# Decay attention into a mixture of experts: handing the expert weights' nine transfers to the scheduler later

## The chip, the core and the metric

One core of one Trainium2 chip runs the whole kernel. The metric is device microseconds of one execution, as the median of several; lower is better. Engines are called PE (matrix products), DVE, ACT and POOL (element-wise work; only DVE and ACT read PE's accumulators), and SP, which issues every transfer of this kernel.

## What is computed

The input is eight batches of eight heads with 576 positions and 64 channels. First comes causal attention with a decay that is added to the scores:

```python
scores = scale * np.matmul(q, k.transpose(0, 1, 3, 2))
log_f = np.log(np.clip(f, 0.0001, 1.0))
cum = np.cumsum(log_f, axis=-1)
decay = cum[:, :, :, None] - cum[:, :, None, :]
scores = np.where(causal, -1000000000.0, scores + decay)
attn = softmax(scores)            # written out in the reference
out = np.matmul(attn, v)
```

The heads of a batch are joined into x (576 x 512), and four experts follow. Each one is causal attention over x with its own matrices; a gate keeps the best two of four per position:

```python
logits = x @ w_gate               # the two largest, softmax over them: w
q, k, v = x @ wq[e], x @ wk[e], x @ wv[e]
a = softmax(where(causal, -1e9, scale * q @ k.T))
out += mask_e * w * (a @ v @ wo[e])
```

## The kernel before

**Pairs.** The unit of work is a pair: two heads of the decay attention (`a`), or two experts (`m`), for one batch. The order is four `a` pairs of batch 0, then for each batch from 1 on its four `a` pairs and the two `m` pairs of the batch before, and at the end two `m` pairs: 48 pairs. Products are made to nearly full precision out of a high and a low part of each operand, `x = h + l`: ACT writes the rounded copy `h`, and DVE or POOL subtracts it from `x` to get `l`.

**Stages of a pair.** `prep_attn` loads k and q, turns them over on PE (L278), and splits them (ACT L286 into tile `kq`, DVE L287 into `ka`). `max_pass` computes all scores once (L439) for the row maxima (DVE L445, L489), turns the maxima over on PE (L494, tile `mp`), copies them out with ACT (L496, tile `ms`) and sends them by two small transfers into row 68 of `kq` (`copy_bits`, L255). `scores` computes them again with that row (L525, L526), takes exponentials on ACT (L545 to L576), zeroes what lies above the diagonal on POOL (L511, L547, L577) and adds up row sums on POOL (L583 to L586, tile `R`). `attend` is L607; `row_sums` and `apply_rows` divide by the sums and split the result into `xh` (ACT L711) and `xl` (DVE L712). Those feed the experts: `moe_front` (L337), `prep_moe` (L413) and at the end of a batch `project_out` (L734).

**The weights.** `load_weights` (L199) brings the experts' matrices in once, in nine steps: two transfers of wv and the small one of w_gate, two of wk, two of wq (L226), two of wo (L221). Each step loads a staging tile `st`, has ACT copy the high part (L229: `vh`, `kh`, `qh`, `oh`) and POOL subtract for the low part (L230: `vl`, `kl`, `ql`, `ol`).

**The order of the work.** A heap (L792 to L803) hands out the steps of all stages by due time in units of pairs: each stage has a start and an end out of the tables `PLAN`, `HEAD`, `TAIL` and `W`, and its steps are spread between them. In that order the instructions are given to the framework's list scheduler, which then sets each engine's own order by its estimate of when operands are there. The weights' task is L791, with start `W["l0"]` and end `W["l1"]`: step i of nine is due at l0 + (l1 - l0) x i / 9. Every engine then runs its list strictly in order; an instruction that waits holds up all behind it. POOL's `memset` of the maxima's tile (L435) waits until PE has turned over the maxima of two pairs before, since there are two buffers.

Of the kernel before, what the change touches and what calls it, by code (L numbers as in the profile page):

```python
# [21 lines left out]
INV_SCALE = 8.0  # L22


W = dict(d1=-1.62, l0=1, l1=4, c0=-1.39, c1=-1.57, x0=-0.76)
PLAN = {
    "a0": dict(prep=(-1.974, -1.27), vals=(-0.214, -0.256), max=(-0.804, -1.205), scores=(0.003, 0.147), attend=(1.121, 1.748)),
    "a1": dict(prep=(-2, -1.228), vals=(-0.415, 1.126), max=(-0.601, -0.643), scores=(-0.269, 0.973), attend=(1.185, 2.238), sums=(1.749, 1.965), apply=(2.392, 2.449)),
# [26 lines left out]
def tile_decay_attention_moe(ctx: ExitStack, tc, q, k, v, f, w_gate, wq, wk, wv, wo, out):  # L55
# [665 lines left out]
    def project_out(grp, b):  # L721
        yh, yl = grp["yh"], grp["yl"]
        wh, wl = wts["o"]

        for blk in [4, 0, 1, 2, 3] if b % 2 else range(4):
            po = ptile(ps_x, "x", f"po{b}_{blk}")
            n = 0
            for a in range(NEP):
                if blk < 4:
                    lh, ll = (y[a][:, 128 * blk : 128 * blk + 128] for y in (yh, yl))  # L730
                else:
                    lh, ll = (y[:, a] for y in last64[0])
                for l, r in ((lh, wh), (lh, wl), (ll, wh)):
                    nc.tensor.matmul(po, l, r[:, a], start=(n == 0), stop=(n == 3 * NEP - 1))  # L734
                    n += 1
            if b < B - 2:
                ob = work.tile([128, DM], F32, tag="outb", name=f"outb{b}_{blk}", bufs=2)
            else:
                ob = xs.tile([128, S], F32, tag="xl", name=f"outb{b}_{blk}")[:, :DM]
            nc.scalar.activation(ob, po, AF.Copy)  # L740
            if blk < 4:
                nc.sync.dma_start(out[b, 128 * blk : 128 * blk + 128], ob)
            else:
                for i in range(2):
                    nc.sync.dma_start(out[b - 1 + i, 512:S], ob[64 * i : 64 * i + 64])
            yield 2.0
# [9 lines left out]
    def task(t0, t1, total, make):  # L756
        tasks.append([t0, len(tasks), t0, t1, total, 0.0, make, None])
# [4 lines left out]
    for i, (kind, b, p) in enumerate(seq):  # L762
# [20 lines left out]
        if p % 2 == 1:  # L783
            task(*at["sums"], 3.0, lambda g=grp, us=us, b=b, kind=kind: row_sums(g, us, b, kind))
            task(*at["apply"], 2.0, lambda g=grp, us=us, b=b, kind=kind, p=p: apply_rows(g, us, b, kind, p - 1))
            if kind == "m":
                task(*at["out"], 10.0, lambda g=grp, b=b: project_out(g, b))
    task(-1.999, W["d1"], 1.0, decay_rows)
    task(W["c0"], W["c1"], 1.0, constants)
    task(W["x0"], W["x0"], 1.0, spread_rows)  # L790
    task(W["l0"], W["l1"], 4.0, load_weights)  # L791
    heap = [tuple(x[:2]) for x in tasks]  # L792
# [31 lines left out]
```

## Time and profile before

| | us |
|---|---|
| median of 3 runs | 768.52 (768.11 to 770.03) |
| the profiled execution's own time | 770.86 |
| its span, first to last instruction | 768.5 |
| PE busy | 726.0 (94% of the span) |
| DVE busy | 586.7 (76%) |
| ACT busy | 471.5 (61%) |
| POOL busy | 406.5 (53%) |

The span is what the trace's times count from; the profiled execution took 2.4 us more than its span, which lie around it. A row of the timeline view gives start, duration, engine, line, what was written from what, and in brackets how long the engine had sat idle and what ended that. SPq rows are issues of transfers, not the transfers themselves. The clock row of this profile prints full speed from the start, so for the first stretch the durations of equal matmuls are the better guide.

### The profile page before, as it was taken

The page shows a single profiled execution, that of the slowest core. Times are in us where ns is not written, and L with a number is a line of the kernel's source. Part 1 is how long each engine was busy: PE and PEld are TensorE (multiplying, and loading weights), DVE is VectorE, ACT ScalarE, POOL GpSimd, SP SyncE. Part 2 cuts the span into 40 slices and gives each one's busy share as a digit, 9 for nine tenths or more (in the row PEclk, how much of TensorE's full clock was granted, in tenths as well). Part 3 has the DMA queues.
Part 4 walks back from the last instruction along what each step waited for, and adds up shares of the span by engine and source line. Part 5 has one row for each costly group of instructions (what it writes and reads, how often), then busy time and mean ns, then how long its engine had stood idle before and what let it go on. Part 6 is the DMA issues. An engine that isn't in the chain of part 4 may idle for free.

```text
span 768.5 us, 16867 instructions
## 1 busy us (share of the span) xinstructions
PE 726.0 (94%) x5704; PEld 592.5 (77%) x5704; DVE 586.7 (76%) x1856; ACT 471.5 (61%) x1151; POOL 406.5 (53%) x770
## 2 busy tenths in 40 slices
PE   4699899999999999999999999999999999999997
PEld 3577589768887788777987778877887879879865
DVE  7678977988688877888778886878777987785733
ACT  5477556767566765676556765667656865555543
POOL 8297644564455564456446544555644564473260
PEclk9999999999999999999999999999999999999999
DMA  8974540544226441365224542265413632202203
GB/s 165 192 146 105 124 107 22 115 92 95 49 49 154 109 109 33 69 147 138 67 53 98 142 110 49 50 144 133 108 33 65 150 88 48 55 19 52 67 15 123
DMA packets 142233, 70.84 MB, mean 92 GB/s; under 512 B 124004, under 2 KB 124484, under 8 KB 142148
## 3 DMA queue, kind: packets, MB, share of 16 engines
q1 hardware_dynamic: 142148, 69.77, 40.3%
q8 instruction: 45, 0.74, 0.4%
q14 instruction: 40, 0.33, 0.1%
HBM read 31.43 MB, written 9.74 MB: 54 GB/s over the span
## 4 chain that ended last, share of the span: by engine, by line
PE 76%; DVE 11%; ACT 4%; DMA 4%; issue 3%; POOL 2%; SPq 0%; DVEq 0%; ACTq 0%
PE pp_m L413 11%; PE ob_a L607 8%; PE pv L337 7%; PE po L734 7%; PE m_a L439 7%; PE s_a L525 6%; PE s_a L526 5%; PE ob_m L607 4%; PE tp_a L278 4%; PE s_m L526 3%; PE s_m L525 3%; PE m_m L439 3%; PE sm_a L650 2%; DVE junk_a L445 2%; DVE ka_a L287 2%
## 5 line engine op out<-in xcount | busy, mean ns | idle before, releaser
L287 DVE TENSOR_TENSOR ka_a<-tp_a,kq 64x288 fp32r<-64x288 f32 x256 | 114.6, 453 | 19.2 <-ACT kq L286 12.6
L286 ACT ACTIVATE kq<-tp_a 64x288 fp32r<-64x288 f32 x256 | 101.1, 403 | 39.7 <-DVE ka_a L287 23.5
L445 DVE CUSTOM_DVE_ANT_0 junk_a<-m_a,mask 128x192 bf16<-128x192 f32 (+2 forms) x192 | 93.5, 487 | 40.8 <-PE m_a L439 22.5
L525 PE MATMUL s_a<-ka_a 128*128 128x320 f32 (+4 forms) x384 | 112.7, 316 | 2.8 <-ACT P_a L545 1.6
L439 PE MATMUL m_a<-kq 128*128 128x320 f32 (+4 forms) x384 | 103.9, 333 | 8.7 <-DVE mxs_a L445 3.9
L526 PE MATMUL s_a<-kq 128*128 128x320 f32 (+4 forms) x384 | 102.2, 298 | 0.5 <-DMA kq<-ms_a 0.5
L420 ACT ACTIVATE kq<-pp_m 64x288 fp32r<-64x288 f32 x128 | 51.8, 405 | 70.9 <-PE pp_m L413 34.8
L547 POOL TENSOR_SCALAR_AFFINE_SELECT P_a<-P_a 128x256 f32<-128x256 f32 x64 | 26.1, 409 | 125.3 <-ACT P_a L545 125.2
L511 POOL TENSOR_SCALAR_AFFINE_SELECT P_a<-P_a 128x128 f32<-128x128 f32 x128 | 42.1, 332 | 82.3 <-ACT P_a L560 80.5
L439 PEld LDWEIGHTS m_a<-kq 128*128 128x128 f32 (+1 forms) x384 | 65.1, 190 | 19.1 <-DVE mxs_a L445 8.0
L525 PEld LDWEIGHTS s_a<-ka_a 128*128 128x128 f32 (+1 forms) x384 | 69.8, 184 | 11.7 <-issue 4.3
L421 DVE TENSOR_TENSOR ka_m<-pp_m,kq 64x288 fp32r<-64x288 f32 x128 | 58.1, 454 | 24.7 <-ACT kq L420 22.2
L583 POOL TENSOR_TENSOR R_a<-P_a 128x448 f32<-128x448 f32 x64 | 73.3, 1145 | 4.2
L526 PEld LDWEIGHTS s_a<-kq 128*128 128x128 f32 (+1 forms) x384 | 69.0, 183 | 2.5 <-DMA kq<-ms_a 0.7
L607 PE MATMUL ob_a<-P_a,va 128*64 128x320 f32 (+1 forms) x512 | 69.2, 412 | 1.0 <-POOL pl L577 1.0
L445 DVE CUSTOM_DVE_ANT_0 junk_m<-m_m,mask 128x192 bf16<-128x192 f32 (+2 forms) x96 | 46.6, 486 | 16.1 <-PE m_m L439 14.2
L525 PE MATMUL s_m<-ka_m 128*128 128x192 f32 (+2 forms) x192 | 56.8, 316 | 0.5 <-ACT P_m L560 0.2
L607 PEld LDWEIGHTS ob_a<-P_a,va 128*64 128x64 f32 x512 | 33.9, 136 | 30.2 <-POOL pl L577 2.3
L584 POOL TENSOR_TENSOR R_a<-R_a,P_a 128x320 f32<-128x320 f32 x64 | 55.0, 864 | 1.0
L526 PE MATMUL s_m<-kq 128*128 128x192 f32 (+2 forms) x192 | 50.6, 295 | 1.9 <-DMA kq<-ms_m 1.8
L439 PE MATMUL m_m<-kq 128*128 128x192 f32 (+2 forms) x192 | 48.0, 310 | 0.0
L337 PE MATMUL pv<-vh,xh_a 128*128 128x260 f32 x160 | 47.6, 297 | 0.0
(190 smaller groups left out, 2065.5 us busy)
## 6 DMA issues: line engine op xcount, KB each, us to landing
ka_a<-kq SPq DMA_DIRECT2D x64, 288.0 KB
kn_a<-in_k_dram SPq DMA_DIRECT2D x64, 144.0 KB
qn_a<-in_q_dram SPq DMA_DIRECT2D x64, 144.0 KB
ka_m<-kq SPq DMA_DIRECT2D x32, 288.0 KB
va<-in_v_dram SPq DMA_DIRECT2D x64, 128.0 KB
out_dram<-outb SPq DMA_DIRECT2D x32, 256.0 KB
kq<-ex SPq DMA_DIRECT2D x94, 9.0 KB
va<-in_v_dram SPq DMA_DIRECT2D x32, 32.0 KB
```

The source lines that it names most:

```text
L286: nc.scalar.activation(hv, src, AF.Copy)
L287: nc.vector.tensor_tensor(lo[:, h, gs], src, hv.bitcast(F32), ALU.subtract)
L337: nc.tensor.matmul(pv[:, :NV], l[c][:, t0 : t0 + 128], r[:, c], start=(n == 0), stop=(n == 3 * KC - 1))
L413: nc.tensor.matmul(pp[:, :HS], w[:, c, es], x[c][:, gs], start=(n == 0), stop=(n == 3 * KC - 1))
L421: nc.vector.tensor_tensor(lo[:, h, gs], src, hv.bitcast(F32), ALU.subtract)
L439: nc.tensor.matmul(dst, qB[0:K, h, i0 : i0 + dst.shape[0]], kB[0:K, h, j0:j1], start=True, stop=True)
L445: nc.vector.tensor_tensor_reduce(jk[:, :n], src, mask[:, MW - n :], 1.0, init, ALU.add, ALU.max, acc)
L525: nc.tensor.matmul(dst, kaf[:, c : c + m], qA[:, h, i0:i1], start=True, stop=False)
L526: nc.tensor.matmul(dst, kqf[0:K, c + h * S : c + h * S + m], qB[0:K, h, i0:i1], start=False, stop=True)
L583: g.tensor_tensor(r[:, h, 128:S], q[:, 320:768], q[:, 768:1216], ALU.add)
L584: g.tensor_tensor(r[:, h, 256:S], r[:, h, 256:S], q[:, 1216:1536], ALU.add)
L607: mm = nc.tensor.matmul(dst[64 * h : 64 * h + 64, c0 : c0 + rhs.shape[-1]], vs[h][0:kp, blk], rhs, start=first, stop=last,)
```

## The change

Two numbers of table `W` change: `l0` from 1 to 1.6, `l1` from 4 to 5.

```diff
-W = dict(d1=-1.62, l0=1, l1=4, c0=-1.39, c1=-1.57, x0=-0.76)
+W = dict(d1=-1.62, l0=1.6, l1=5, c0=-1.39, c1=-1.57, x0=-0.76)
```

So the nine steps are due at 1.60, 1.98, 2.36, 2.73, 3.11, 3.49, 3.87, 4.24 and 4.62 pairs, where they were due at 1.00, 1.33, 1.67 and so on to 3.67. Nothing is added or removed. The scheduler's lists change on every engine well beyond the weights: on PE the first difference is at the 26th row and the last near row 1,870 of some 3,780; behind that all engines' lists are the same.

**First place: SP and ACT in the first pairs.** Tiles are named with stage, pair within its batch and a running number. On SP, ahead of and behind the two transfers of pair 0's row maxima (`kq_111<-ms_a_0`), before:

```order
L226 DMA st_v_540<-in_moe_wv_dram 128x8x64
L255 DMA ka_a_2_354<-kq_113 64x2x576
L306 DMA va_104<-in_v_dram 128x4x64 x2
L311 DMA va_104<-in_v_dram 64x2x64
L306 DMA va_105<-in_v_dram 128x4x64
L255 DMA ka_a_2_354<-kq_113 64x2x576
L306 DMA va_105<-in_v_dram 128x4x64
L311 DMA va_105<-in_v_dram 64x2x64
L226 DMA st_v_600<-in_moe_wv_dram 128x8x64
L255 DMA kq_111<-ms_a_0_303 1x5x128 x2
L226 DMA st_v_659<-in_moe_w_gate_dram 128x4x4
L226 DMA st_k_705<-in_moe_wk_dram 128x8x64
```

and now:

```order
L306 DMA va_104<-in_v_dram 128x4x64
L255 DMA ka_a_2_354<-kq_113 64x2x576
L306 DMA va_104<-in_v_dram 128x4x64
L311 DMA va_104<-in_v_dram 64x2x64
L306 DMA va_105<-in_v_dram 128x4x64 x2
L255 DMA ka_a_2_354<-kq_113 64x2x576
L311 DMA va_105<-in_v_dram 64x2x64
L226 DMA st_v_639<-in_moe_wv_dram 128x8x64
L255 DMA kq_111<-ms_a_0_303 1x5x128 x2
L226 DMA st_v_695<-in_moe_wv_dram 128x8x64
```

One transfer of wv instead of two now stands ahead of the maxima's. On ACT, around the copy of pair 0's maxima (`ms_a_0`) and its first exponentials (`P_a_0`), before:

```order
L286 ACTIVATE kq_114<-tp_a_3_586 64x288
L229 ACTIVATE vh<-st_v_540 128x4x128
L286 ACTIVATE kq_114<-tp_a_3_616 64x288
L496 ACTIVATE ms_a_0_303<-mp_a_0_301 10x128
L229 ACTIVATE vh<-st_v_600 128x4x128
L229 ACTIVATE vh<-st_v_659 128x4x4
L545 ACT_TABLE_LOAD
L545 ACTIVATE P_a_0_316<-s_a_0_318 128x512
L229 ACTIVATE kh<-st_k_705 128x4x128
L545 ACTIVATE P_a_0_316<-s_a_0_333 128x512
```

and now:

```order
L286 ACTIVATE kq_114<-tp_a_3_580 64x288
L286 ACTIVATE kq_114<-tp_a_3_606 64x288
L496 ACTIVATE ms_a_0_303<-mp_a_0_301 10x128
L229 ACTIVATE vh<-st_v_639 128x4x128
L545 ACT_TABLE_LOAD
L545 ACTIVATE P_a_0_316<-s_a_0_318 128x512
L229 ACTIVATE vh<-st_v_695 128x4x128
L229 ACTIVATE vh<-st_v_767 128x4x4
L545 ACTIVATE P_a_0_316<-s_a_0_333 128x512
```

The first `vh` went from ahead of `ms_a_0` to behind it, and the second and third from ahead of the first exponential to between the first and the second.

**Second place: POOL and DVE when batch 0's first results are split.** On POOL, the row sums of pair 3 (`R_a_3`) and the weights' low parts among them, before:

```order
L577 AFFINE_SELECT pl_108<-pl_108 64x128
L584 TENSOR_TENSOR R_a_3_959<-R_a_3_959,P_a_3_958 128x320 x2
L230 TENSOR_TENSOR ol<-st_o_1013,oh 128x512
L585 TENSOR_TENSOR R_a_3_959<-R_a_3_959,P_a_3_958 128x192 x2
L230 TENSOR_TENSOR ol<-st_o_1056,oh 128x512
```

and now:

```order
L577 AFFINE_SELECT pl_108<-pl_108 64x128
L584 TENSOR_TENSOR R_a_3_949<-R_a_3_949,P_a_3_948 128x320 x2
L435 MEMSET mxs_a_2_1301 64x2
L585 TENSOR_TENSOR R_a_3_949<-R_a_3_949,P_a_3_948 128x192
L230 TENSOR_TENSOR ql<-st_q_1020,qh 128x4x128
L585 TENSOR_TENSOR R_a_3_949<-R_a_3_949,P_a_3_948 128x192
L586 TENSOR_TENSOR R_a_3_949<-R_a_3_949,pl_108 64x2x64
L230 TENSOR_TENSOR ql<-st_q_1094,qh 128x4x128
```

A `memset` now stands behind the first two additions, and the two `ql` come where one `ol` was (the two `ol` follow later). On DVE, ahead of the second split (`xl_a_0_1`), before:

```order
L712 TENSOR_TENSOR xl_a_0_0_974<-ot_a_0_632,xh_a_0_0_973 128x576
L287 TENSOR_TENSOR ka_a_1_870<-tp_a_1_997,kq_112 64x288
L694 TENSOR_TENSOR ot_a_1_679<-cp_a_0_1020,ot_a_1_679 128x288
L287 TENSOR_TENSOR ka_a_2_926<-tp_a_2_946,kq_113 64x288
L712 TENSOR_TENSOR xl_a_0_1_1024<-ot_a_1_679,xh_a_0_1_1023 128x576
```

and now:

```order
L287 TENSOR_TENSOR ka_a_1_860<-tp_a_1_987,kq_112 64x288
L445 ISA junk_a_0_946,mxs_a_0_878<-m_a_0_944,mask 128x320
L445 ISA mxs_a_0_878 128x1
L489 TENSOR_REDUCE mxs_a_0_878<-mx_a_0_933 64x2
L712 TENSOR_TENSOR xl_a_0_1_1008<-ot_a_1_671,xh_a_0_1_1007 128x576
```

The second split now follows the last reduction of the maxima `mxs_a_0`, which POOL's `memset` of `mxs_a_2` waits for by way of PE.

## Rows read from the trace of the kernel before

**Rows 1.** Busy time of each engine in stretches of 20 us (windows view): stretch, its length, busy us and instructions of PE, PE's weight loads, DVE, ACT and POOL, then PE's clock row, the share of the 16 transfer engines in use and GB/s.

```profile
0.00:20.00 20.00, 9.12 (x42) 7.38 (x43) 15.13 (x37) 9.92 (x23) 16.80 (x43) 1.00 0.90 167
20.00:40.00 20.00, 13.98 (x51) 10.81 (x51) 10.94 (x40) 9.38 (x21) 5.47 (x9) 1.00 1.07 190
40.00:60.00 20.00, 19.31 (x140) 14.19 (x139) 15.97 (x53) 14.28 (x37) 18.04 (x32) 1.00 0.76 152
60.00:80.00 20.00, 18.86 (x157) 14.09 (x156) 17.45 (x41) 14.01 (x35) 15.88 (x28) 1.00 0.46 104
80.00:100.00 20.00, 15.74 (x117) 11.10 (x117) 18.54 (x54) 12.51 (x30) 10.12 (x19) 1.00 0.51 105
...
120.00:140.00 20.00, 20.00 (x180) 18.11 (x178) 16.41 (x55) 11.16 (x27) 9.71 (x17) 1.00 0.14 32
140.00:160.00 20.00, 18.60 (x162) 13.96 (x158) 18.17 (x58) 14.17 (x37) 13.28 (x26) 1.00 0.55 121
```

**Rows 2.** PE's timeline from 23 to 38 us.

```profile
23.88 0.71 PE L278 MATMUL tp_a<-ident,kn_a 96*128 96x96 f32 x3 [2.18 <-DMA kn_a<-in_k_dram]
...
26.95 0.37 PE L494 MATMUL mp_a<-ident,mxs_a 128*10 128x128 f32 x1 [0.17 <-DVE mxs_a L489]
...
29.08 1.06 PE L439 MATMUL m_a<-kq 128*128 128x192 f32 x3 [1.19 <-ACT ms_a L496]
30.79 0.98 PE L439 MATMUL m_a<-kq 128*128 128x448 f32 x2 [0.65 <-DVE mxt_a L456]
...
37.23 0.58 PE L525 MATMUL s_a<-ka_a 128*128 128x256 f32 x1 [0.58 <-ACT P_a L545]
```

**Rows 3.** ACT's timeline from 27 to 38 us.

```profile
27.95 0.63 ACT L229 ACTIVATE vh<-st_v 128x512 fp32r<-128x512 f32 x1 [2.06 <-DMA st_v<-in_moe_wv_dram]
28.48 0.39 ACT L286 ACTIVATE kq<-tp_a 64x288 fp32r<-64x288 f32 x1
28.77 0.25 ACT L496 ACTIVATE ms_a<-mp_a 10x128 fp32r<-10x128 f32 x1
32.83 0.88 ACT L229 ACTIVATE vh<-st_v 128x512 fp32r<-128x512 f32 x2 [3.81 <-DMA st_v<-in_moe_wv_dram]
35.28 1.28 ACT L545 ACT_TABLE_LOAD   x1 [1.58 <-PE s_a L526]
...
37.59 0.59 ACT L545 ACTIVATE P_a<-s_a 128x512 f32<-128x512 f32 x1
```

**Rows 4.** SP's issues from 21 to 31 us (timeline).

```profile
21.43 0.69 SPq L226 DMA_DIRECT2D st_v<-in_moe_wv_dram  x1
...
29.14 0.60 SPq L226 DMA_DIRECT2D st_v<-in_moe_wv_dram  x1
29.84 1.64 SPq L255 DMA_DIRECT2D kq<-ms_a  x2
```

**Rows 5.** Issues by transfer, with the size of one (transfer view).

```profile
st_v<-in_moe_wv_dram SPq DMA_DIRECT2D x2, 256.0 KB
```

**Rows 6.** DVE's timeline from 77 to 83 us.

```profile
77.08 3.54 DVE L712 TENSOR_TENSOR xl_a<-ot_a,xh_a 128x576 fp32r<-128x576 f32 x1 [0.26 <-ACT xh_a L711]
80.65 1.42 DVE L287 TENSOR_TENSOR ka_a<-tp_a,kq 64x288 fp32r<-64x288 f32 x3
```

**Rows 7.** All executions of the line L712 (source view): count, then the shortest, median and longest in ns.

```profile
L712 DVE TENSOR_TENSOR xl_a<-ot_a,xh_a x32: 742/750/3539, 74.4 to 692.4; 128x576 fp32r<-128x576 f32 x32
```

**Rows 8.** POOL's timeline: one row at 60 us, then 75 to 83 us.

```profile
60.49 0.09 POOL L435 MEMSET mxs_a<- 64x2 f32 x1 [1.09 <-PE mp_a L494]
...
75.98 1.68 POOL L584 TENSOR_TENSOR R_a<-R_a,P_a 128x320 f32<-128x320 f32 x2
77.63 1.26 POOL L230 TENSOR_TENSOR ol<-st_o,oh 128x512 fp32r<-128x512 f32 x1
78.85 1.14 POOL L585 TENSOR_TENSOR R_a<-R_a,P_a 128x192 f32<-128x192 f32 x2
82.13 1.26 POOL L230 TENSOR_TENSOR ol<-st_o,oh 128x512 fp32r<-128x512 f32 x1 [2.14 <-ACT oh L229]
```

**Rows 9.** PE's timeline from 81 to 84 us.

```profile
81.59 0.41 PE L439 MATMUL m_a<-kq 128*128 128x320 f32 x1 [1.16 <-ACT kq L286]
82.22 0.44 PE L278 MATMUL tp_a<-ident,qn_a 96*128 96x96 f32 x3 [0.22 <-DVE ka_a L287]
83.64 0.39 PE L525 MATMUL s_a<-ka_a 128*128 128x256 f32 x1 [0.98 <-ACT P_a L545]
```

**Rows 10.** ACT's timeline from 81 to 82 us.

```profile
81.13 0.41 ACT L286 ACTIVATE kq<-tp_a 64x288 fp32r<-64x288 f32 x1 [3.50 <-DVE ka_a L287]
81.44 0.62 ACT L229 ACTIVATE oh<-st_o 128x512 fp32r<-128x512 f32 x1
```

**Rows 11.** All executions of the small DVE line L672 (source view), as in Rows 7.

```profile
L672 DVE TENSOR_TENSOR zt_a<-rc_a,zt_a x16: 191/196/1153, 63.9 to 685.4; 128x18 fp32r<-128x18 f32 x16
```

**Rows 12.** POOL's timeline at 64 us.

```profile
63.87 1.14 POOL L583 TENSOR_TENSOR R_a<-P_a 128x448 f32<-128x448 f32 x1
```

**Rows 13.** First uses of the weights on PE (source view): after the counts and durations come the start of the first and of the last execution.

```profile
L337 PE MATMUL pv<-vh,xh_a x160: 279/283/388, 98.4 to 722.5; 128*128 128x260 f32 x160
...
L413 PE MATMUL pp_m<-xh_a,qh x128: 290/296/401, 113.5 to 716.0; 128*128 128x288 f32 x128
...
L734 PE MATMUL po<-oh,yh_m x64: 391/398/502, 236.3 to 763.9; 128*128 128x512 f32 x64
```

**Rows 14.** Two matmuls of the same shape in PE's timeline, at 40 and at 100 us.

```profile
40.22 0.57 PE L526 MATMUL s_a<-kq 128*128 128x448 f32 x1
...
100.54 0.37 PE L526 MATMUL s_a<-kq 128*128 128x448 f32 x1
```

## The prediction

> **What bounds the kernel now.** I read the windows view first, to see where PE has time to lose. From 100 us on there is next to none: PE is busy for all of 120 to 140, and 1.4 us short of full from 140 to 160, the worst later stretch of this size until the end of the program comes near [rows 1]. So a saving has to come out of the first 100 us, where PE is idle for 10.9, 6.0, 0.7, 1.1 and 4.3 us of five stretches of 20 [rows 1]. The reader should see two holes in this: one from 20 to 40, where transfers are saturated (190 GB/s, and the share of the engines in use is over 1), and one from 80 to 100, where transfers are at half and DVE is busy 18.5 us of 20. The first 20 us come ahead of all that the change touches.
>
> I read the first hole in the PE timeline and then asked each releaser what held it. PE waits 2.18 us for pair 3's k, which was issued before any weights and is not touched. Then it waits 1.19 us for `ms_a`, 0.65 for a DVE reduction, 0.58 for the first exponential [rows 2]. `ms_a` is the copy of pair 0's maxima on ACT. Its input was turned over on PE at 26.95 and took 0.37, so it was there at 27.32 [rows 2], but ACT started it at 28.77, because ACT had stood 2.06 us on the first transfer of wv, until 27.95, and the weight copy and a queued split came first [rows 3]. That is a weight which nobody reads before 98.4 us [rows 13], standing in front of the work that PE is waiting for.
>
> The second hole has another cause. DVE's split `xl_a` at 77.08 took 3.54 us [rows 6]; the median of its 32 executions is 0.75 [rows 7]. POOL added two-operand tiles without a gap from 75.98 to 79.99 meanwhile, one of the additions being the low part of a weight, `ol` [rows 8], and the split ended 0.63 us after POOL stopped. The small L672, median 0.196, shows the same thing: its longest execution is 1.15 us, starting at 63.9 [rows 11], under a POOL addition from 63.87 to 65.01 [rows 12]. A DVE operation with two operands in SBUF gets little through while POOL runs such operations back to back. Behind that split ACT sat idle for 3.50 us until DVE's next release [rows 10], and PE lost 1.16, 0.22 and 0.98, together 2.36 us [rows 9].
>
> **The change, part by part.** The sum is against the profiled execution, 770.86 us; the median of the runs is 768.52, 2.34 lower, and I carry the difference over unchanged. No instruction is added or removed; only places change.
>
> *The maxima of pair 0.* `ms_a` now stands ahead of all weight copies on ACT. Its input is there at 27.32, so it starts some 1.4 us earlier (28.77 less 27.35, with ACT's queued split done by then). That removes PE's 1.19 us wait [rows 2]. The row then has to reach `kq`: its two transfers were issued at 29.84, behind two wv transfers of 256 KB [rows 4, 5]. One of the two is now behind them. At 190 GB/s [rows 1] 256 KB is 1.38 us, and an issue of 0.69 on SP goes too [rows 4], so the landing moves by about as much as PE does, and the scores follow. I take **-1.2 us**. The ends: 0, if the removed wait comes back one step later (first rival below), and -2.4, if the waits of 0.65 and 0.58 behind it close as well (1.19 + 0.65 + 0.58). I take the row that is directly released, since the other two have releasers of their own: DVE has to reduce what PE makes, and the exponential needs its table load of 1.28 us whatever the weights do [rows 3].
>
> One rule speaks against this part. The Trainium skill (DMA: Bandwidth & Descriptors, Rules for kernel authors) says to issue a transfer early, compute, and wait for it late, so that its fixed cost overlaps. By that rule alone issuing later gains nothing, and this term would be 0 and the forecast 767.0. The trace does not agree here: the wait was not late, it stood on ACT 70 us before the weight's first use [rows 3, 13].
>
> *The copies that moved to between the exponentials.* The second and third `vh` now stand ahead of the second exponential instead of the table load. They cost ACT 0.88 us [rows 3]; one `kh` stood in that place before, 0.62 by the equal copy `oh` [rows 10]. The difference, 0.3 us, lies in front of one exponential, whose accumulator PE wanted 0.58 us late already [rows 2]; I count it into the bounds.
>
> *The split under POOL's run.* `xl_a_0_1` now stands right behind the last reduction of `mxs_a_0`, and POOL's `memset` of `mxs_a_2`, which needs PE to have turned those same maxima over, is now behind the first two additions. A memset of this line waited 1.09 us for just that at 60.49 [rows 8]. So POOL's run is cut there, and the split can be held at most by the two additions, 1.68 us [rows 8], where it lost 2.79 before (3.54 less 0.75) [rows 6, 7]. Between nothing and 1.68 I take the middle, 0.84, a saving of 1.95 us on DVE. PE turned 2.79 us of DVE's loss into 2.36 of its own [rows 9], so this is 1.65 for PE; I take **-1.5 us**. The ends are -2.36, all of that idle time, and +2.4, worked out under the rivals.
>
> *What now lies from 70 to 90 us.* Two `qh`, 0.62 each by the equal `oh` [rows 10], come onto ACT in addition, and two `ql` of 1.26 each, by the equal `ol`, onto POOL [rows 8]. ACT was idle for 3.50 us there [rows 10] and POOL for 2.14 [rows 8], so I cost them at **0**. If the split's wait goes, ACT's idle time shrinks to some 1.6 us (3.50 less 1.95), which still covers 1.24; without any cover it is +1.24. The wq transfers go out where the transfer engines are at 46% [rows 1], and the first wq is read at 113.5, wo at 236.3 [rows 13], some 30 us and far more after their splits: **0**.
>
> *The rest of the lists.* They differ up to the middle of the program. PE's idle time in a stretch of 20 us there goes from 0 to 1.4 [rows 1], and I have no reason for a sign: **0**, with 1.0 either way.
>
> The sum is -1.2 - 1.5 = **-2.7 us**, so 768.16 for an execution like the profiled one and **765.8** as the median.
>
> **The rivals.**
>
> *The wait moves along.* ACT stands on the second and third `vh` in front of the second exponential instead. The first wv transfer took 6.5 us from issue (21.43) to ACT's start (27.95), the second 3.7 (29.14 to 32.83) [rows 3, 4]. If the later ones take as long as the first, the second exponential, due about 36, waits a microsecond or more and eats the 1.2. For it: the transfer engines stay saturated to 40 us. Against: one transfer fewer lies ahead, and two wq leave this stretch. It gives -1.5, 767.0.
>
> *The split is held as long as before.* POOL's run and the split meet as they did, and only the first term stays: -1.2, 767.3. For it: POOL still has the additions of pair 3 to do when the split is due. Against: the cut by the memset.
>
> *The run grows: slower than before.* If PE has the maxima turned over before POOL gets to the memset, nothing cuts the run, and it is now longer: two additions (1.68), one more (0.57), `ql` (1.26), another (0.57), a short one, `ql` (1.26), some 5.7 us with the short one taken as 0.4, where the split met 2.91 us of a run before (77.08 to 79.99) [rows 8]. It decides at the point where the split starts within the first two additions and both `qh` are there in time. The split then loses some 2.8 us more, at PE's rate (2.36 of 2.79) +2.4; with the first term -1.2 that is +1.2, 769.7, and with the lists' 1.0 against it 770.7; without the first term 770.9.
>
> *More goes than I count.* The first term at 1.2, all of 2.36 in the second, and PE's clock rising sooner. A 448-column matmul of scores takes 0.57 us at 40 and 0.37 at 100 [rows 14]: PE runs at the 1.2 GHz level until then, after a stretch full of gaps, and at 2.4 behind it. The Trainium skill (TensorE: Matmul & The Clock Gate, Part 1) has it that half rate is the resting state and activity lifts it; by that rule a denser stretch around 30 us would bring the rise forward. The rows show one rise only and cannot say. ACT's exponentials would soon bind in its place; I allow 1.1. That gives -4.7, 763.8.
>
> That the change does nothing is no case: the lists show the transfers moved.
>
> **How the numbers follow.** Chances: the forecast 0.40, the wait that moves 0.15, the split as before 0.16, the longer run 0.17, more than counted 0.12. A measurement of this kernel tells about 0.3%, 2.3 us, from no change, so faster means under 766.2 and slower over 770.8. The forecast with its spread of about 1 us lies under 766.2 in 0.28 of its 0.40; the last rival adds its 0.12 and the two middle ones 0.05: faster **0.45**. Slower is half of the longer run, 0.09, and 0.03 of the middle ones in bad luck with the lists: **0.12**. The rest is **0.43** within 0.3%. The range goes from 763.2, under the last rival's value, to 769.9, over the longer run's value: what is left out is the part of the longer run without the first term and some luck at both ends, together under 0.2. The forecast alone would have 764.6 to 767.0.
>
> **What would show it.** In the changed kernel's profile ACT's `ms_a` of pair 0 should start near 27.4 without a wait for `st_v` ahead of it, and PE's 1.19 us wait for it be gone; pair 0's scores should follow some 1.2 us sooner. The longest `xl_a` should be under 2.4 us, PE's idle time from 80 to 100 us near 2.8 instead of 4.3, and the work behind the middle of the program the same, only shifted. The forecast is wrong if ACT waits over 1 us for `st_v` in front of an exponential, if the longest `xl_a` stays at 3 us or more, or if PE's idle time between 100 and 400 us grows by more than a microsecond.

## The result: slower, by 0.8%

The changed kernel took 774.83 us (median of four executions, 774.14 to 775.86), the kernel before in the same session 768.42 (four, 768.11 to 770.03). The ratio is 1.0080, with a 95% interval of 1.0062 to 1.0098. That is slower, 9.0 us over the 765.8 forecast and above the top of the range. The median of the kernel before moved between 768.4 and 771.5 us from one session to the next, so below only ratios within a session are compared.

### The profile after

The profiled execution took 774.14 us, its span is 772.4 (before: 770.86 and 768.5). The change's is the fastest of its four, and that of before is slower than any of its four, so the two spans lie 3.9 us apart where the medians lie 6.4. Read the windows first, against [rows 1]:

```profile
20.00:40.00 20.00, 14.87 (x54) 11.71 (x53) 11.31 (x42) 9.23 (x20) 4.62 (x9) 1.00 1.07 194
60.00:80.00 20.00, 17.81 (x144) 12.54 (x143) 18.48 (x47) 12.49 (x31) 14.64 (x27) 1.00 0.32 76
80.00:100.00 20.00, 16.86 (x114) 12.05 (x115) 17.47 (x54) 13.00 (x29) 12.66 (x21) 0.91 0.66 132
160.00:180.00 20.00, 17.53 (x132) 13.13 (x132) 17.93 (x57) 13.04 (x33) 9.46 (x18) 1.00 0.44 96
320.00:340.00 20.00, 18.61 (x142) 14.20 (x139) 16.62 (x54) 13.54 (x35) 10.79 (x23) 1.00 0.57 132
```

PE is busier from 20 to 40 us, as forecast. From 80 to 100 its busy time rose from 15.74 to 16.86, but with three matmuls fewer (114 for 117): the clock row, the granted clock, says 0.91, where it said 1.00 before. And there are holes of 2.5 and 1.4 us at 160 and at 320, far behind the moved transfers (before: 1.2 and 0.8).

**The head did what was forecast.** ACT after, 27 to 35 us, against [rows 3]:

```profile
27.49 0.27 ACT L496 ACTIVATE ms_a<-mp_a 10x128 fp32r<-10x128 f32 x1
31.73 0.63 ACT L229 ACTIVATE vh<-st_v 128x512 fp32r<-128x512 f32 x1 [3.98 <-DMA st_v<-in_moe_wv_dram]
33.67 1.28 ACT L545 ACT_TABLE_LOAD   x1 [1.31 <-PE s_a L526]
34.97 0.60 ACT L545 ACTIVATE P_a<-s_a 128x512 f32<-128x512 f32 x1
35.46 0.73 ACT L229 ACTIVATE vh<-st_v 128x512 fp32r<-128x512 f32 x2
```

`ms_a` starts at 27.49 (28.77 before). ACT still stands on a wv transfer, even longer, but nothing that PE needs is behind it.

**The split did not.** The split view's row of before was [rows 7]; after, the longest of the 32 is 4.49 us:

```profile
L712 DVE TENSOR_TENSOR xl_a<-ot_a,xh_a x32: 739/753/4487, 70.8 to 697.6; 128x576 fp32r<-128x576 f32 x32
```

DVE, POOL and PE after, from 75 to 85 us, against [rows 6, 8, 9]:

```profile
75.27 4.49 DVE L712 TENSOR_TENSOR xl_a<-ot_a,xh_a 128x576 fp32r<-128x576 f32 x1
79.68 1.42 DVE L287 TENSOR_TENSOR ka_a<-tp_a,kq 64x288 fp32r<-64x288 f32 x3
```

```profile
75.09 1.70 POOL L584 TENSOR_TENSOR R_a<-R_a,P_a 128x320 f32<-128x320 f32 x2
76.73 0.10 POOL L435 MEMSET mxs_a<- 64x2 f32 x1
76.78 0.59 POOL L585 TENSOR_TENSOR R_a<-R_a,P_a 128x192 f32<-128x192 f32 x1
77.33 1.27 POOL L230 TENSOR_TENSOR ql<-st_q,qh 128x512 fp32r<-128x512 f32 x1
78.56 0.58 POOL L585 TENSOR_TENSOR R_a<-R_a,P_a 128x192 f32<-128x192 f32 x1
79.22 0.85 POOL L586 TENSOR_TENSOR R_a<-R_a,pl 64x128 f32<-64x128 f32 x1
84.18 1.28 POOL L230 TENSOR_TENSOR ql<-st_q,qh 128x512 fp32r<-128x512 f32 x1 [4.12 <-ACT qh L229]
```

```profile
75.30 0.28 PE L494 MATMUL mp_a<-ident,mxs_a 128*10 128x128 f32 x1 [0.38 <-DVE mxs_a L489]
...
80.67 0.47 PE L278 MATMUL tp_a<-ident,qn_a 96*128 96x96 f32 x3 [2.35 <-DVE ka_a L287]
...
84.49 0.57 PE L439 MATMUL m_a<-kq 128*128 128x448 f32 x1
85.00 1.14 PE L650 MATMUL sm_a<-R_a,ones_col 128*32 128x288 f32 x8
```

The split starts 0.18 us into POOL's run and is let go when the run pauses, at 79.14. The memset at 76.73 stands in the run without any idle time in front of it: PE had turned the maxima over by 75.58. PE stands 2.35 us, and a little later 448 columns take 0.57 us, as at 40 us, and not 0.37 [rows 14]: PE had fallen to the 1.2 GHz level behind the gap. Most of what is lost here is that clock: from 72 to 92 us PE's waits add up to 3.99 us where they were 3.56, and 0.91 over 20 us is 1.8 us less of full speed (an estimate from the clock row).

**The same thing happens in places that the prediction never named.** POOL, DVE, ACT and PE after, 154 to 160 us:

```profile
154.92 1.68 POOL L584 TENSOR_TENSOR R_m<-R_m,P_m 128x320 f32<-128x320 f32 x2
156.55 0.09 POOL L435 MEMSET mxs_a<- 64x2 f32 x1
156.60 1.13 POOL L585 TENSOR_TENSOR R_m<-R_m,P_m 128x192 f32<-128x192 f32 x2
```

```profile
155.77 2.02 DVE L672 TENSOR_TENSOR zt_a<-rc_a,zt_a 128x18 fp32r<-128x18 f32 x1
...
158.30 0.78 DVE L675 STREAM_TRANSPOSE rr_a<-zt_a 128x576 f32<-128x576 f32 x1
```

```profile
159.12 0.68 ACT L676 ACTIVATE rt_a<-rr_a 128x576 fp32r<-128x576 f32 x1 [0.41 <-DVE rr_a L675]
```

```profile
159.85 0.40 PE L693 MATMUL cp_a<-rt_a,sel 128*128 128x288 f32 x1 [0.87 <-ACT rt_a L676]
```

A subtraction of 18 elements per partition, 0.19 us in the median, takes 2.02 us, and PE waits for what comes of it.

**It is POOL in every trace.** Over the traces of both kernels and the fourteen experiments below, DVE runs the split `xl_a` 505 times. Of the 307 that start while POOL does nothing none takes over 0.76 us, of the 20 that start under one of POOL's maskings none over 0.86. Of the 178 that start under a POOL addition or subtraction 166 take over 0.9, up to 4.49.

### A ledger of where the time goes

Idle time alone does not add up here: PE's idle time over the whole span went down, from 42.5 to 41.6 us, while its busy time rose by 4.8. So I matched every matmul of a kernel with the same matmul of the profiled run before and took the difference of their starts. Where the order differs, the matmuls that now stand ahead and did not before are taken out, at the spacing their kind has in the trace of before. The table holds the median of that lag in us (positive is later), for the matmuls that start within 15 us from the time at the left (time in the trace of before). The experiments' names are told below.

| from | change | e1 | e2 | e3 | e4 | g2 | g3 | g4 | g5 | m1 | m2 | m3 |
|---|---|---|---|---|---|---|---|---|---|---|---|---|
| 45 | -1.0 | -1.2 | -0.2 | -1.4 | -1.0 | -1.1 | 0.1 | -0.3 | 0.0 | 0.8 | -1.1 | -1.5 |
| 60 | -0.8 | 0.3 | -0.3 | -1.3 | -1.3 | -0.9 | 0.4 | -0.1 | 0.0 | 0.8 | -1.0 | -1.3 |
| 75 | 1.3 | 0.9 | -0.4 | 1.9 | 0.0 | 1.6 | -0.9 | -1.0 | -2.5 | -1.0 | 1.8 | -3.0 |
| 90 | 1.1 | 0.7 | -2.1 | 0.9 | -1.3 | 1.7 | -1.8 | -2.9 | -2.5 | 0.5 | 3.4 | 1.8 |
| 150 | 1.2 | 0.8 | -0.1 | 6.4 | -0.8 | 1.0 | -1.2 | -3.1 | -2.5 | 1.5 | 3.6 | 3.8 |
| 165 | 2.9 | 1.0 | 1.6 | 7.3 | 1.7 | 1.3 | 2.1 | -2.8 | -2.4 | 2.1 | 5.3 | 6.3 |
| 210 | 2.8 | 1.0 | 1.5 | 7.3 | 1.6 | 1.2 | 2.0 | -2.9 | -2.4 | 0.7 | 5.8 | 6.3 |
| 225 | 4.2 | 1.1 | 2.8 | 7.4 | 3.0 | 2.4 | 3.4 | -1.8 | -2.3 | 0.7 | 7.0 | 6.3 |
| 300 | 3.6 | 1.0 | 2.4 | 6.6 | 2.7 | 1.9 | 2.9 | -2.5 | -2.3 | 0.4 | 7.3 | 6.7 |
| 345 | 5.9 | 0.1 | 5.3 | 5.8 | 7.2 | 6.3 | 5.8 | 1.8 | -2.7 | -0.4 | 6.9 | 5.9 |
| 405 | 5.5 | 0.1 | 4.8 | 5.8 | 6.7 | 5.8 | 5.3 | 1.3 | -2.7 | -0.4 | 6.9 | 5.9 |
| 720 | 5.2 | -0.3 | 5.1 | 5.7 | 6.0 | 6.0 | 5.3 | 1.5 | -3.1 | -1.2 | 6.8 | 5.9 |
| 735 | 3.9 | -1.6 | 3.7 | 4.4 | 4.7 | 6.0 | 3.9 | 0.1 | -4.4 | -2.6 | 5.5 | 4.6 |

The change wins 1.0 at the head, loses 2.1 at 75 us (-0.8 to 1.3), 1.7 at 156, 1.4 at 225 and 2.3 between 300 and 345, and gets back some 1.0 in between: 5.5 at 405, from where the order is that of before. Of the last step, at 730 us, the change has nothing: there the profiled run of before lost 1.3 us. The table compares single executions, so its last row holds the 3.9 us between the two spans and not the 6.4 between the medians.

### The profile page after: what moved, and what is told of

It reads as the page before. It is cut to its first block, busy times and chain, and to the rows that moved or that the text cites. A ratio compares the mean times of both kernels' runs of the same rounds, so it can differ in the third digit from the quotient of the medians.

```text
span 772.4 us, 16858 instructions
## 1 busy us (share of the span) xinstructions
PE 730.8 (95%) x5704; PEld 594.4 (77%) x5704; DVE 591.7 (77%) x1856; ACT 471.7 (61%) x1151; POOL 407.7 (53%) x770
## 4 chain that ended last, share of the span: by engine, by line
PE 47%; DVE 4%; ACT 2%; issue 1%; POOL 1%; DMA 1%; SPq 0%; DVEq 0%; ACTq 0%
PE pp_m L413 7%; PE po L734 6%; PE ob_a L607 4%; PE pv L337 4%; PE ob_m L607 3%; PE m_a L439 3%; PE s_a L525 3%; PE s_a L526 3%; PE s_m L525 2%; PE s_m L526 2%; PE tp_a L278 2%; PE m_m L439 2%; PE sm_a L650 1%; PE oa_m L607 1%; DVE junk_m L445 1%
## 5 line engine op out<-in xcount | busy, mean ns | idle before, releaser
L526 PE MATMUL s_a<-kq 128*128 128x320 f32 (+4 forms) x384 | 104.1, 301 | 1.0 <-DMA kq<-ms_a 1.0
```

The source lines that it names most:

```text
L526: nc.tensor.matmul(dst, kqf[0:K, c + h * S : c + h * S + m], qB[0:K, h, i0:i1], start=False, stop=True)
```

## The experiments

**Theory H**: operations of DVE with all their operands in SBUF are held while POOL adds; a new order makes new meetings, and the loss is where PE waits behind one. Rivals: **S**, the split at 75 us alone; **E**, the transfers and copies moved to later places, as such; **O**, the new order of PE's own rows, holds or not; **N**, for an experiment that took another form of the operation, that this form is held as well.

### One half of the change at a time, and two other pairs of values

```diff
-W = dict(d1=-1.62, l0=1.6, l1=5, c0=-1.39, c1=-1.57, x0=-0.76)
+W = dict(d1=-1.62, l0=1.6, l1=4, c0=-1.39, c1=-1.57, x0=-0.76)    # e1
+W = dict(d1=-1.62, l0=1, l1=5, c0=-1.39, c1=-1.57, x0=-0.76)      # e2
+W = dict(d1=-1.62, l0=1.6, l1=5.4, c0=-1.39, c1=-1.57, x0=-0.76)  # e3
+W = dict(d1=-1.62, l0=1.3, l1=4.5, c0=-1.39, c1=-1.57, x0=-0.76)  # e4
```

> l0=1.6 with l1=4 left as it was: the first half of the change alone. The order differs from that of before only between 33 and 90 us; behind 90 us every engine has the order of before. Theory H (VectorE's operations whose operands all lie in SBUF are held while GpSimd runs its additions; the time is set by which of them are held where TensorE waits): the early gain of 1.1 us stays, the split of pair 0 stands behind a shorter run of additions, and the rest is that of before: 767.3 (766.3 to 768.8). Rival S (the whole loss is the split at 75 us and TensorE's lower clock behind it): the same 767.3 if the longest xl_a of the batch stays under 3.6 us. Rival E (what costs is the early part itself, the weights' transfers and copies moved behind the maxima): 772 or more.

> l1=5 with l0=1 left as it was: the second half of the change alone. The order of the first 33 us is that of before; from about 133 us on it is that of the change. Theory H: no early gain, the held row-sum operation near 156 us (2.02 us in the change) and the held split near 318 us are met again: 772.5 (770.5 to 776). Rival S: as the change if a split of the first batch takes over 4 us (775), as before if none does (768.5). Rival E: 768.5.

> l0=1.6 with l1=5.4: the order is that of the change to about 82 us, so the split of pair 0 is held by the same run of GpSimd as in the change (over 4 us), and from 172 us on it is that of before. Theory H: the loss at the split is there and half of it is given back by 110 us, what the change lost at 156 us and behind is not: 769.5 (768 to 771.5). Rival S: 774.8, as the change. Rival E: 774.8.

> l0=1.3 with l1=4.5: GpSimd's run of additions by the split of pair 0 is cut by its masks, so that split should take under 3 us; from about 147 us on the order is that of the change. Theory H: the early gain is kept, and what the change lost at 156 and 318 us is lost again: 771.5 (770 to 774). Rival S: 767.3. Rival E: 774.8.

Measured, as ratio to before: e1 1.0009 (0.9994 to 1.0023), e2 1.0077 (1.0056 to 1.0098), e3 1.0089 (1.0071 to 1.0107), e4 1.0056 (1.0038 to 1.0074). e1 takes the time of the kernel before, and H's 767.3, a ratio of 0.998 to the 768.5 that it was reckoned from, is missed: the early gain of 1.2 is lost at 64.78, where a row sum is held 1.96 us. So the whole loss comes with l1, and E falls for the first transfers, which e1 moves too; for the later ones g4 below decides. e2 and e4 lie in the ranges written down for H. S falls by e2: no stand at 75 us, no lower clock, a ledger of -2.1 at 90 us, and yet the loss of the change, from 150 us on. H missed e3 by nearly 6 us (1.0013 reckoned): it has the order of before from 172 us, as I had reckoned, and nothing is lost there. But between 82 and 172 us its order is neither's, and it meets two holds of its own. DVE and PE of e3:

```profile
143.41 1.75 DVE L378 TENSOR_TENSOR gt<-gt,sm 128x20 f32<-128x20 f32 x1
...
160.50 1.90 DVE L672 TENSOR_TENSOR zt_a<-rc_a,zt_a 128x18 fp32r<-128x18 f32 x1
```

```profile
145.22 0.59 PE L384 MATMUL pg<-gt,ident 128*32 128x5 f32 x32 [1.66 <-DVE gt L378]
```

The first stands in PE's way. The second does not by these rows: PE's only longer stand there, 1.31 us, ends at 160.63, as that hold begins, after a copy and an addition on DVE that took 0.60 and 0.83 us instead of some 0.18. In that stretch the ledger goes from 0.9 at 90 us to 7.3 at 165. The two stands are 3.0 of that; behind each the clock row falls to 0.83 (140 to 150 and 160 to 170 us), which is 3.4 us less of full speed (an estimate from that row).

### Another form of the held operations

f1 writes DVE's split as a scalar_tensor_tensor; f2 the row sums' operations too; f3 is f2's edit in the kernel before.

```diff
-nc.vector.tensor_tensor(l, x, h.bitcast(F32), ALU.subtract)
+nc.vector.scalar_tensor_tensor(l, x, 1.0, h.bitcast(F32), ALU.mult, ALU.subtract)
```

> The change, with VectorE's splits (L712, 64 of them) written as scalar_tensor_tensor, x*1.0 - h, in place of tensor_tensor, x - h. The order on TensorE, ScalarE, GpSimd and SP is that of the change row for row, and on VectorE too but for the operation's kind. Theory H (operations of VectorE with all operands in SBUF are held while GpSimd adds, and the loss is where they are held; this form is not held): all 32 xl_a at 0.75 us or near it, the 2.35 us stand of TensorE at 78 to 81 us gone and with it the stretch at the lower clock behind it, the held splits at 130, 185 and 318 us gone; the row sums (2.02 us at 156 us) stay held: 770.5 (768.5 to 772.5). Rival N (this form is held just as much): 774.8, with the long splits where they were. Rival O (held operations are beside the point, the order of TensorE's own rows costs the time): splits short, 774.8 all the same.

> The change, with the splits as in f1 and the three small operations of the row sums (L665, L671, L672: adding 1e-9, copying, subtracting) written as scalar_tensor_tensor too. The order is that of the change to 243 us, and behind that but for about 240 of TensorE's 4,714 rows. Theory H: no operation of VectorE at these lines is held, and what the change lost against before at 75, 156, 185 and 306 to 318 us is gone: 767.5 (765.5 to 769.5). Rival N: 774.8. Rival O: 774.8.

> The kernel before, with the same two edits (splits and row sums as scalar_tensor_tensor). The order is that of before but for 16 of TensorE's rows near 735 us. Theory H: what before itself loses to held operations (the split of 3.54 us at 77 us, where TensorE stood less than a microsecond, and one row-sum operation or split for each batch, most of which cost TensorE little) comes back: 767.5 (765.5 to 769). Rivals N and O: 769.0, as before.

Measured: f1 1.0059 (1.0039 to 1.0080), f2 1.0121 (1.0085 to 1.0156), f3 1.0035 (1.0012 to 1.0057). N holds, H's numbers fail. The split of f1 is held as long as in the change, to the hundredth, and its ledger follows the change's within 0.2 us all the way:

```profile
L712 DVE SCALAR_TENSOR_TENSOR xl_a<-ot_a,xh_a x32: 736/754/4491, 71.0 to 697.6; 128x576 fp32r<-128x576 f32 x32
```

f2 is slower than the change. Its three small operations together are some 0.02 us longer in the median, and in three later batches (at 425, 515 and 605 us) one of them lies under a POOL addition, where in the change it passed:

```profile
425.68 1.18 DVE L672 SCALAR_TENSOR_TENSOR zt_a<-rc_a,zt_a 128x18 fp32r<-128x18 f32 x1
```

f3 has the same 1.18 us in five batches. In f2 the three cost PE about 1 us (ledger, 405 to 620 us), which is the smaller part of what it loses to the change, and behind 243 us some of PE's rows stand elsewhere, so it is not shown that the 0.02 us alone put them there. f2 also prices the lower clock. To 75 us it runs as the change does, in the same order and with the same hold, but its clock from 80 to 100 us is lower:

```profile
80.00:100.00 20.00, 16.98 (x104) 11.76 (x105) 16.81 (x50) 12.29 (x27) 12.42 (x20) 0.83 0.64 132
```

0.83 against 0.91, and 0.98 us more lag from there on.

### The held operation taken from DVE

ScalarE copies instead. Where that stands for a subtraction the low part is not computed, so these four kernels serve to find the cause and are of no other use. The order on PE is the change's (g2), the change's but for rows between 80 and 147 us (g3, g4), or that of before but for three rows (g5).

```diff
-nc.vector.tensor_tensor(z[:, :, 1], rc, zt[:, :, 0], ALU.subtract)
+if nm in ('_a1_2',): nc.scalar.activation(z[:, :, 1], rc, AF.Copy)                # g2, g4
+else: nc.vector.tensor_tensor(z[:, :, 1], rc, zt[:, :, 0], ALU.subtract)
...
-nc.vector.tensor_tensor(l, x, h.bitcast(F32), ALU.subtract)
+if (nm, p) in (('_a0_0', 1),): nc.scalar.activation(l, x, AF.Copy)                # g3, g4, g5
+else: nc.vector.tensor_tensor(l, x, h.bitcast(F32), ALU.subtract)
```

(g2 and g4 have such a line for `_a3_0`'s split and for L671 of `_a2_0` and `_a3_0` too.)

> The change, with four of VectorE's held operations behind 150 us done by ScalarE instead (a copy from SBUF): the row sums' subtraction of pairs 2 and 3 of batch 1 (held 2.02 us at 156 us in the change), the row sums' copy of pairs 0 and 1 of batches 2 and 3 (0.97 at 216, 1.62 at 307) and the second split of pairs 0 and 1 of batch 3 (1.62 at 318). Two of the four leave out a subtraction, so the low part of those values is not computed. The order on TensorE, GpSimd and SP is that of the change row for row, and VectorE and ScalarE differ by these four alone. Theory H (the loss behind 150 us is made where GpSimd's additions hold VectorE): TensorE's wait of 0.87 us at 160 us is gone, and of what the change lost at 156 to 165 us (2.4 us) and at 306 to 345 us (1.9) most comes back: 771.2 (769.8 to 772.6). Rival O (the new order of TensorE's own rows costs it, held operations or not): 774.8 (773.8 to 775.8).

> The change, with the one split that was held for 4.49 us at 75 us (pairs 0 and 1 of batch 0, second tile) done as a copy by ScalarE, so its low part is not computed. The order is that of the change to 80 us and again from 147 us on; between them some rows stand elsewhere. Theory H: TensorE's stand of 2.35 us at 78 to 81 us and the 3.41 us at the lower clock behind it are gone, but half of that had been given back by 110 us, and the loss behind 150 us stays: 772.8 (771.3 to 774.2). Rival S (the split alone is the cause): 768.5. Rival O: 774.8.

> g2 and g3 together: the five held operations with the longest holds before 350 us (but for one split at 130 us and one at 185 us) done by ScalarE. Theory H: 769.3 (767.5 to 771). Rival S: as g3, 768.5. Rival O: 774.8.

> The kernel before, with the second split of pairs 0 and 1 of batch 0 (held 3.54 us at 77 us there) done as a copy by ScalarE, low part not computed. The order is that of before but for three rows of TensorE. Theory H: TensorE found work under most of that hold, so little comes back: 768.0 (766.8 to 769.2). If every held microsecond counted: 765.7.

Measured: g2 1.0068 (1.0046 to 1.0091), g3 1.0049 (1.0032 to 1.0066), g4 0.9989 (0.9970 to 1.0008), g5 0.9963 (0.9944 to 0.9983). f1, which runs as the change does, had 1.0059 in its session and the change 1.0080 in its own, so across sessions a ratio is good to some 0.002. g4's 0.0070 to 0.0091 is far over that: with both groups of holds away the loss is gone, though the transfers are the change's and PE's order too from 147 us on. Its ledger says how: -2.8 at 165 us where the change has 2.9. So H stands against O for the front, and E falls there too. H does not account for all of the rest: g4 too loses at 225 us and between 300 and 345. And part of g4's gain is one that the kernel before could have had as well, as g5 shows below: against g5, in the same session, g4 is still 2.0 us slower (medians 770.38 and 768.38). g3 came as H had it (772.8 is a ratio of 1.0056 to the 768.5 it was reckoned from). g2 is 2.5 us short of H. Its edit at 156 us works; ACT of g2, against the row at 159.12 above, now has `rt_a` without a wait:

```profile
157.53 0.68 ACT L678 ACTIVATE rt_a<-rr_a 128x576 fp32r<-128x576 f32 x1
```

and the ledger at 165 is 1.3 where the change has 2.9. But what it won there it lost by 345 us, in a stretch where the clock row falls to 0.91 while the change's is at 1.00:

```profile
320.00:340.00 20.00, 17.55 (x130) 13.22 (x128) 16.67 (x54) 11.68 (x31) 11.78 (x24) 1.00 0.60 138
340.00:360.00 20.00, 19.67 (x141) 14.35 (x140) 12.75 (x40) 12.43 (x29) 8.96 (x18) 0.91 0.41 98
```

g5 missed H's 768.0 and came as the other number written down, 765.7 (a ratio of 0.9964) if every held microsecond counted: it gains 2.5 us at 75 us, nearly all of the 2.79 by which the hold exceeds the median [rows 6, 7], and it keeps them to the end. (The edit takes the split's own 0.75 us from DVE as well.) PE of g5 waits 0.34 us where before it waited 1.16, 0.22 and 0.98 [rows 9]; it is busy for 17.71 us from 80 to 100 [rows 1]:

```profile
81.16 0.39 PE L525 MATMUL s_a<-ka_a 128*128 128x256 f32 x1 [0.34 <-ACT P_a L545]
```

```profile
80.00:100.00 20.00, 17.71 (x131) 13.05 (x131) 18.50 (x57) 13.56 (x33) 10.66 (x22) 1.00 0.52 110
```

### The remainder at 300 to 345 us, and a complete kernel without the hold

```diff
+if (nm, p) in (('_a0_0', 1),): nc.gpsimd.tensor_tensor(l, x, h.bitcast(F32), ALU.subtract)  # m1: in before; m3: in the change
+if (nm, p) in (('_m0_0', 1),): nc.scalar.activation(l, x, AF.Copy)                           # m2: in the change
```

> The kernel before, with the second split of pairs 0 and 1 of batch 0 computed by GpSimd instead of VectorE: the whole computation, nothing left out. The order is that of before up to 84 us and again from 212 us. Theory H: VectorE is not held at 77 us (2.5 us in the profiled run of g5), GpSimd's run grows by one split of about 1.4 us, and other holds may arise between 84 and 212 us: 768.0 where before has 770.0 (a ratio of 0.9974; 0.995 to 1.000). Rival O (the split's place does not matter): a ratio of 1.000.

> The change, with one split of batch 0's MoE (second pair) done as a copy by ScalarE, its low part not computed; what it serves here is the order: that of the change up to 193 us, with the split held 4.49 us at 75 us and the row sum held 2.02 us at 156 us, and that of before from 243 us on. Theory H with a remainder (the loss by 210 us is made by those two holds, 2.9 to 3.2 us at TensorE, and the 1.7 to 2.2 us that were lost once more at 315 to 345 us, with four holds there taken away too, belong to that stretch's own order): a ratio to before of 1.0042 (1.002 to 1.006), and TensorE's lag flat from 245 us on. If the remainder were carried over from the front and only showed late: a ratio of 1.007 to 1.008.

> The change, with the second split of pairs 0 and 1 of batch 0 computed by GpSimd: the whole computation, nothing left out. The order is that of the change to 85 us and that of before from 172 us on. Theory H: the early gain of 1.1 us is kept, the hold at 75 us with TensorE's stand of 2.35 us and the lower clock behind it are gone, and the loss behind 315 us too; what holds arise between 85 and 172 us decides the rest: a ratio to before of 0.997 (0.993 to 1.002). If the loss of the change lay in the later transfers themselves: 1.006 or more.

Measured: m1 0.9969 (0.9952 to 0.9986), m2 1.0057 (1.0041 to 1.0074), m3 1.0060 (1.0042 to 1.0078). **m1 beats both kernels**, by 0.3% the kernel before, and it leaves nothing out: POOL does the split itself, in the run that used to hold it (behind an inserted line the experiments' line numbers are one to three higher):

```profile
L712 POOL TENSOR_TENSOR xl_a<-ot_a,xh_a x1: 1432/1432/1432, 80.2 to 80.2; 128x576 fp32r<-128x576 f32 x1
```

It gives 2.4 us where g5 gave 2.9, because a later row sum is held in turn (its copy, L671, takes 1.57 us at 89.53): the ledger goes from -1.0 to 0.5 at 90 us, with the clock row at 0.83 from 90 to 100. m2 is flat from 255 to 330 us (7.3), so the 2.3 us that the change loses between 300 and 345 do not come from the front; they belong to the order of that stretch. Its ratio lies midway between the two that were written down (1.0042, and 1.007 to 1.008); its front lost more than I had put there, the clock row being at 0.74 from 80 to 100 us. m3 is the miss that teaches most. H had 0.997, and 1.0060 is also what was written down for the case that the later transfers cost the time; the trace tells the two apart. The split's hold is gone, the ledger stands at -3.0 at 75 us, and then POOL's next run of additions catches another operation. DVE, POOL and PE of m3, and its window:

```profile
88.33 4.03 DVE L672 TENSOR_TENSOR zt_a<-rc_a,zt_a 128x18 fp32r<-128x18 f32 x1
```

```profile
88.47 1.12 POOL L583 TENSOR_TENSOR R_a<-P_a 128x448 f32<-128x448 f32 x1
89.55 1.66 POOL L584 TENSOR_TENSOR R_a<-R_a,P_a 128x320 f32<-128x320 f32 x2
91.18 1.13 POOL L585 TENSOR_TENSOR R_a<-R_a,P_a 128x192 f32<-128x192 f32 x2
```

```profile
93.70 0.74 PE L439 MATMUL m_a<-kq 128*128 128x448 f32 x1 [4.86 <-DVE mxt_a L456]
```

```profile
80.00:100.00 20.00, 13.94 (x93) 9.14 (x94) 14.93 (x35) 8.75 (x21) 11.80 (x21) 0.83 0.58 117
```

An operation of 0.19 us stands for 4.03, PE for 4.86, the ledger goes from -3.0 to 1.8, and the clock falls behind it.

## Why the prediction was wrong

*The maxima of pair 0, -1.2.* Right: the ledger has -1.0 at 45 us, and the wait of 1.19 is gone. Some of it came back at the first exponential (PE waits 1.01 us for `P_a` at 35.62, 0.58 before), but not as the first rival had it: that exponential follows the table load, and the two `vh` behind it start without a wait for their transfer.

*The split under POOL's run, -1.5.* This step failed. It rested on one sentence: the memset of `mxs_a_2` needs PE to have turned the maxima over, so it cuts the run. I had taken a wait at another place (1.09 us at 60.49 [rows 8]) for one here. PE was done, the memset waited for nothing, and the split met the run 0.18 us after its start. The trace of before shows in a place that I had not read that such a memset let nothing go there: the second longest of its splits, under additions with a memset among them:

```profile
690.22 2.21 DVE L712 TENSOR_TENSOR xl_a<-ot_a,xh_a 128x576 fp32r<-128x576 f32 x1
```

```profile
690.62 0.09 POOL L435 MEMSET mxs_m<- 64x2 f32 x1
```

What came is the third rival in kind, the split within the first two additions and no cut, but with one of its conditions unmet: only the first `qh` was there in time, and POOL waited 4.12 us for the second (84.18 above). So the run that held the split was 4.05 us to its pause and not 5.7, and the split lost 0.95 us more than before and not 2.8. That the rival's price, +2.4, lies near the +2.1 of the ledger is luck: most of the 2.1 is by the estimate above the lower clock behind the gap, which neither that rival nor the forecast had.

*The rest of the lists, 0 with 1.0 either way.* This step cost more: +4.3 us between 150 and 405 (1.2 to 5.5), and by e2 it is the loss of the change even where the split is not held. "I have no reason for a sign" was wrong, for the reason stood in my own rows. I had read L712 and L672 as being held by POOL [rows 7, 8, 11, 12] and treated that as a fact of two places, while the change reorders DVE and POOL over 360 us, and DVE has such operations in every batch. The runs show how such an order is redrawn: 2.02 us at 156 us in the change, 3.27 at 126 in e2, 1.75 and 1.90 in e3, 4.03 in m3. The order of before has few of them in PE's way; a new one meets what it happens to meet. That there is more to lose than to gain by it is a reading of these few runs and not shown: m1 has another order than before from 96 to 213 us and is faster. Of the prediction's own signs of being wrong two came: the longest `xl_a` is over 3 us, and PE's idle time between 100 and 400 us grew from 6.8 to 8.5. What the term should have held besides is the order of ACT's list, told below.

*What lies from 70 to 90 us, 0.* Half right: the first `qh` found ACT idle. One of the `ql` stood in the run that held the split, 1.27 us of it, as an `ol` of 1.26 did before [rows 8].

*What was left open.* The step of 1.4 us at 225 us comes in every kernel that has the change's order there, and is still there where ACT took the row sum's copy at 216 us (g2, g4). The one longer wait of PE's that the change has there and before has not comes from ACT's order. ACT of before, then ACT and PE of the change:

```profile
229.66 0.25 ACT L496 ACTIVATE ms_m<-mp_m 10x128 fp32r<-10x128 f32 x1
229.93 0.41 ACT L286 ACTIVATE kq<-tp_a 64x288 fp32r<-64x288 f32 x1
```

```profile
233.18 0.41 ACT L286 ACTIVATE kq<-tp_a 64x288 fp32r<-64x288 f32 x1
233.62 0.27 ACT L496 ACTIVATE ms_m<-mp_m 10x128 fp32r<-10x128 f32 x1
```

```profile
233.94 0.78 PE L439 MATMUL m_m<-kq 128*128 128x192 f32 x3 [0.56 <-ACT ms_m L496]
```

The copy of the maxima stands behind a split now, as at the head of the kernel before, and none of DVE's operations from 226 to 235 us is held. So 0.56 of the 1.4 us is made by the order of ACT's rows, which none of the rivals names; where the other 0.8 goes is open. That of 2.3 at 300 to 345 also stays when two holds there are taken away. m2 shows that the second belongs to that stretch; which wait makes it was not settled. The change waits there for ACT as well (0.58 at 323.60, 0.21 at 326.55), again with no operation of DVE held from 321 to 328 us, where before waits 0.16. In e2, where the clock stays up, PE's waits of over 0.15 us from 316 to 348 us add up to 2.35 (the longest 1.11 on the transfer from `ms_m` to `kq`), before to 1.10, so they carry 1.3 of the 2.9 that e2 loses there. How often an execution falls to the lower clock was not controlled either. Within a kernel a mean granted clock lower by 0.001 goes with some 0.6 us more (an estimate over all executions on record). The mean is 0.996 for the change's four and 0.997 for 79 of before, but 0.999 for g4 and g5 and 0.992 to 0.994 for e3, m2 and m3, so the ratios of these hold a microsecond or more of clock, one way or the other.

## What to carry to other kernels

Before you move work between rows, list the operations that another engine can hold (here: DVE with its operands in SBUF, under POOL's additions): one such row in the profile is a property of the kind and not of the place. Price a reorder of many rows with a range of its own and not with zero, for it redraws every such meeting. To gain, take the operation away from the engine that is held and give it to the one that holds it, and read the new order for the next such meeting, as m3 shows.

## What the hardware showed that I had not expected

- A held operation is held by the whole run and not by one operation of it: 4.49 us under six of POOL's in a row, a memset among them, 4.03 in m3. It was let go where the run paused for 0.08 us (79.14 to 79.22). The Trainium skill (SBUF — State Buffer, Summary: rules for kernel authors) says that, where a VectorE operation has two inputs in SBUF and the GpSimd operation reads SBUF, the second one to issue fully blocks until the first finishes. The first half agrees. By the second the split would have been held to the end of the first addition, some 0.7 us; the trace has 3.74 over the median, and it decides.
- Of VectorE's small operations the copy of 18 elements is held as well (1.62 us at 307 us in the change, by L671), with a single input; a reciprocal of the same shape next to it never was, nor a transposition of the split's shape, nor the subtraction with one operand in PE's accumulators. Over all sixteen traces 25, 162 and 2,061 of these started under a POOL addition or subtraction, and the longest took 0.27, 0.78 and 0.46 us. In the change:

```profile
L666 DVE RECIPROCAL rc_a<-rc_a x16: 246/266/268, 63.4 to 689.3; 128x18 f32<-128x18 f32 x16
...
L675 DVE STREAM_TRANSPOSE rr_a<-zt_a x16: 759/778/780, 65.9 to 691.6; 128x576 f32<-128x576 f32 x16
...
L287 DVE TENSOR_TENSOR ka_a<-tp_a,kq x256: 387/453/464, 8.1 to 647.9; 64x288 fp32r<-64x288 f32 x128
```

- A gap of PE costs more than its length when PE falls to the 1.2 GHz level behind it: 0.98 us between f2 and the change (clock rows 0.83 and 0.91), with the same order and the same gap. It may be why two savings were worth more together than one by one (against the change's 1.0080: g2 0.0012, g3 0.0031, g4 0.0091), though part of that lies within what sessions differ by; g2 has a clock row of 0.91 at 340 us, and g4 one from 320 to 340.
